# Linear attention and gated MLP on one core: a weight fold cut into quarters and queued behind products, and one load of raw weights moved

## The chip, the cores and the metric

The kernel runs on one core of a Trainium2 chip. The metric is the device time of one execution in microseconds (us). Before the change three runs gave 2350.81, 2344.51 and 2345.13 us, with a median of 2345.13 us.

## The reference

For an input `x` of 2048 rows by 1024 columns, all in 32-bit floats:

```python
xn = layernorm(x)
q, k, v = heads(xn @ wqkv)                       # 32 heads of 32
pq, pk = per_head(q @ w_phi), per_head(k @ w_phi)
phi(p) = concat(softmax(p), softmax(-p))         # 64 features a head
kv, z = phi(pk)^T v, sum_s phi(pk)
s = heads_back(phi(pq) kv / (phi(pq) z + 1e-6)) @ wo
g = silu((sigmoid(xn @ w_gate) * (xn @ w_up)) @ w_down)
out = x + s * g
```

The per-head matrices `w_phi` can be multiplied into the weights of q and k before the projection. The kernel calls this a **fold**: the product of a block of raw weights (`wqkT`) with a block-diagonal matrix made of `w_phi` (`bd`).

## The kernel before, in words

Every large product is cut into two by two blocks and done with seven block products in place of eight (`B11, B21, T2, T3, T4, T1, B22`, in this order); their operands are sums and differences of blocks. Each float is split into a high and a low part, so that one block product is three matmuls (`mm3`, lines L224 to L226; the startup's own lines are L1007). `split` makes the parts: a cast on ScalarE (L219, in the startup L928), then a subtraction on VectorE (L220, in the startup L931).

The 2048 rows are done in two chunks (`c` 0 and 1). Each chunk projects v, then k, then q, seven products each, and then does the gate and up products. One projection product is four tiles of rows (`u` 0 to 3) with 12 matmuls of 128 x 512 each; results pile up in four PSUM banks and are evacuated by `proj_out` (L506 on VectorE, L509 and L512 on ScalarE), which stores the finished ones with L503. The buffer of finished v tiles of T4 has two halves, so a third evacuation waits for the first store to land, and so on.

The startup is written out by hand as a long list of steps (`FIRST`). It covers the layer norm, the folds of k for the quarters k = 0, 1, 2 of the inner dimension, and the first five products of v in chunk 0 (B11 to T4). VectorE carries its evacuations, subtractions and sums in one queue.

The other five folds (k's fourth, and q's four) are put on the list `side`, whose entries are taken one for each tile of a projection product, from v's T1 on. A fold is done by `fold`: four loads of raw weights of 256 KB (L323), four groups of four 128 x 128 matmuls (`fold_products`, L329) into banks 4 to 7 (`bank_102` to `bank_105` in the listings), four copies out of PSUM on ScalarE (`fold_copy`: L339 for k, L337 for q), three stores of plain blocks to DRAM (`fold_keep`, L350), four sums on VectorE and GpSimd (`fold_sum`, L79), and four stores of sums. The raw weights lie in four buffers; a load waits until the group that read its buffer before is done. A projection product then loads its weights from DRAM (`prep`, L469, 1 MB, two buffers in turn) and splits them.

A scheduler places the instructions of the five engines' queues where it expects their inputs to be ready, so the written order binds only through data and through `tc.issue_after`, which keeps what stands under it behind a given instruction. SyncE (SP) issues all DMAs, in one queue.

Of the kernel before, what the change touches and what calls it, by code (L numbers as in the profile page):

```python
# [138 lines left out]
def hedgehog_glu_kernel(  # L139
# [176 lines left out]
    fraw = Ring(halves(43, 11))  # L316
    fblock = {K: Ring(((4, 5), (6, 7), (52, 53), (50, 51))), Q: Ring(((52, 53), (50, 51)))}

    folds, folded = {}, {}

    def fold_load(which, k, n, r=None):
        r = folds[which, k, n] = fraw.next() if r is None else r
        last_sp[:] = [nc.sync.dma_start(r, wqkT[which, n // 2, k + 4 * (n % 2)].rearrange("p g n -> p (g n)")).ins]  # L323
# [28 lines left out]
    def fold(which, k):  # L352

        for n in range(4):
            if (which, k, n) not in folds:
                fold_load(which, k, n)
        for n in range(4):
            fold_copy(which, k, n, fold_products(which, k, n, tps.next()))
        fold_keep(which, k, False)
        if k < 3:  # L360
            for n in range(4):
                fold_load(which, k + 1, n)
        for i in range(4):
            fold_sum(which, k, i, (vector, pool)[i % 2])
        with tc.issue_after(last_sp[0]):
            fold_keep(which, k, True)
# [84 lines left out]
    def prep():  # L451
        if flow["item"] == len(items):
            return False
        n, size = items[flow["item"]]
        if flow["made"] + size - flow["used"] > NW:
            return False
        w = 28 + flow["made"] % NW
        flow["item"] += 1
        flow["made"] += size
        kind, c, what, i = ops[n]  # L460
        if kind == "proj":
            h = len(ready[n]) // 2
            if h == 0:
                here = c == 0 and what == V
                proj_src[n] = r = v_first[i] if here else proj_raw.next()
                if what == V and i in (B11, B21, T4) and not (here and i != T4):
                    nc.sync.dma_start(row4(r), v_block(*{B11: (0, 0), B21: (0, 1), T4: (1, 1)}[i]))
                elif not here:
                    nc.sync.dma_start(row4(r), wf_d[what, i])  # L469
            o = run(w, 2)  # L470
            split((o[:, :, 0], o[:, :, 1]), slots[proj_src[n] + h])
            ready[n] += [w, w + 1]
            return True
        u = units.index((c, *what))
        if i == glu_order[0]:
            if u % (2 * NJ) == 0:
                glu_load(u)
            if (u + 1) % (2 * NJ):
                glu_load(u + 1)
            glu_sums(u)  # L480
        kept = ws_d[u % (2 * NJ), summed.index(i)] if i in summed else None
        if c and i in summed:
            last_sp[:] = [nc.sync.dma_start(slots[w].bitcast(F32), kept).ins]
        else:
            split(pair(w), wraw[u][i])
            if i in summed:
                nc.sync.dma_start(kept, slots[w].bitcast(F32))
        ready[n].append(w)
        return True
# [328 lines left out]
        if q:  # L818
            e_load(u)

    last_mm = []

    def numerators(tp_):

        sums = []
# [231 lines left out]
        pass  # L1057
    for n in range(4):
        fold_load(K, 3, n)
    side.append(lambda: None)  # L1060
    for w, k in [(K, 3)] + [(Q, k) for k in range(4)]:
        side.append(lambda w=w, k=k: fold(w, k))

    gmm = Ring(banks[:4])
    gbank = {}
# [57 lines left out]
    for n, (kind, c, what, i) in enumerate(ops):  # L1123
        ws = ready[n]
        if kind == "proj":
            if n < 5:
                continue
            for u in range(4):
                if i in opening:
                    pbank[u] = pmm.next()  # L1130
                xo = run(XO[i], 4)
                us = slice(u * P, (u + 1) * P)
                for k in range(4):
                    mm3(pbank[u], (xo[:, k, 0, us], xo[:, k, 1, us]), pair(ws[k]),
                        i in opening and k == 0, k == 3, skip_group_check=True)
                step()
                if c and operands.left:
                    operands.step()
            flow["used"] += 4
            while prep():  # L1140
                pass
            store_now(n)
            if c == 0 and what == Q and i == B11:
                block("p", 36, 3, F32R)
            assert what != Q or not c or not proj1.left and not operands.left
            for u in range(4):
                proj_out(c, what, i, u, pbank[u])
                if c == 0 and what == Q:
                    background(last_evac[0], early_k)
                elif c and not (what == V and i in (B11, B21)):  # L1150
                    if what != Q and u < 3 and proj1.left:
                        background(last_evac[0], proj1)
                    elif what == Q and i not in (B11, B21):
                        background(last_evac[0], late_k)
            continue

        j, s = what
        u = units.index((c, j, s))
        if (j, s, i) == (0, 0, 0):
            step(1000)  # L1160
        if i in opening:
            gbank[i] = gmm.next()
        bank = gbank[{B21: B11, T4: T3, B22: T1}.get(i, i)]
        w = [h.rearrange("p (k m) -> p k m", m=P) for h in pair(ws[0])]
        xo = run(XO[i], 4)
        for k in range(4):
            mm3(bank, (w[0][:, k], w[1][:, k]), (xo[:, k, 0], xo[:, k, 1]),
                i in opening and k == 0, k == 3, skip_group_check=True)
        flow["used"] += 1
        while prep():  # L1170
            pass
        last_unit = u == len(units) - 1
        if flow["item"] == len(items) and flow["made"] - flow["used"] < NW:
            hfree.append(ws[0])
            if last_unit and i == 0:
                wfree.extend(range(16, 20))
            while wfree and down_prep():
                pass
        if i == B11:
            u1, u2 = ur.next(), ur.next()  # L1180
            nc.scalar.copy(u1, bank)
        elif i == T2:
            v = nc.vector.tensor_add(u1, u1, bank)
        elif i == T3:
            v = nc.vector.tensor_add(u2, u1, bank)
        else:
            q = {B21: 0, T1: 3, T4: 2, B22: 1}[i]
            if s == 0:
                gates[q] = gates_free.popleft()
            g = gates[q]  # L1190
            if s == 0:
                if q == 0:
                    nc.scalar.activation(g, bank, AF.Sigmoid)  # L1193
                else:
                    v = nc.vector.tensor_add(g, u2 if q == 3 else u1, bank)
                    nc.scalar.activation(g, g, AF.Sigmoid)
            else:
                if q == 0:
                    nc.vector.tensor_mul(g, g, bank)
                else:  # L1200
                    b = u1 if q == 1 else u2
                    v = nc.vector.tensor_add(b, u2 if q == 3 else u1, bank)  # L1202
                    last_pool[:] = [pool.mul(g, g, b).ins]
                if q != 1:
                    later(n + 1 + (q > 0), h_d[(B11, None, B21, T4)[q], j, :, c], g)
                else:

                    a11, a21, a12, a22 = [gates[q] for q in range(4)]
                    s3, s2, s4 = [hs_r.next() for _ in range(3)]
                    pool.sub(s3, a11, a21)  # L1210
                    pool.add(a21, a21, a22)
                    pool.sub(s2, a21, a11)
                    pool.sub(s4, a12, s2)
                    for o, b in ((T3, s3), (T1, a21), (T2, s2), (B22, s4)):
                        later(n + 3, h_d[o, j, :, c], b)
                    gates_free.extend((a22, a11, a12, a21))

        store_now(n + 100 * (n == len(ops) - 1))
        m = (u % (2 * NJ)) * 7 + glu_order.index(i)
        if m > 1:  # L1220
            if c:
                paced(v.ins, beside1, 186 - m)
            elif early_k.left:
                background(v.ins, early_k)
            elif kv_due:
                kv_products()
            else:
                paced(v.ins, beside0, 187 - m)
        if c == 0 and u % (2 * NJ) == 2 * NJ - 1:
            for _ in range((1, 2, 2, 1, 1, 1, 1)[glu_order.index(i)]):  # L1230
                operands.step()
            if i == B22:
                block("p", 36, 3, F32R)
# [211 lines left out]
```

## Time and profile before

| | |
|---|---|
| median of three runs | 2345.13 us (2344.51 to 2350.81) |
| the profiled execution's own time | 2345.94 us |
| its span, from first to last instruction | 2343.9 us |
| TensorE (PE) busy | 2326.3 us, 99% of the span |
| VectorE (DVE), GpSimd (POOL), ScalarE (ACT) busy | 1636.9, 1111.7, 955.6 us |
| share of PE in the chain that ended last | 90% |

PE is busy nearly throughout, so the places to read are the few in which it waits. "Waits" lists sum what an engine waited for; the "chain" follows the work that ended last, step by step; the "timeline" shows instructions with start, duration and, in brackets, the idle time before them and what ended it. Matmul durations in the timeline overlap: the step from one to the next is 0.23 us at full clock.

### The profile page before, as it was taken

The numbers are of one execution on the slowest core, as the hardware profiler recorded it, in microseconds if no ns is written. First come the engines' busy times: TensorE is split into PE (matmuls) and PEld (weight loads), VectorE is DVE, ScalarE is ACT, GpSimd is POOL, SyncE is SP. The second block draws the span as 40 slices with busy tenths as digits, with TensorE's granted clock in tenths as the row PEclk, the third lists the DMA queues.
The fourth block names the chain that finished last, engine by engine and source line by source line (L and its number), as shares of the span: only waits on it lengthen the run. The fifth ranks groups of instructions, "written<-read, shape, count | busy, mean of one in ns | idle before, by whom it ended". The sixth has DMA issues, their size and how long they took to land.

```text
span 2343.9 us, 32067 instructions
## 1 busy us (share of the span) xinstructions
PE 2326.3 (99%) x10644; PEld 1922.1 (82%) x10644; DVE 1636.9 (70%) x2333; ACT 955.6 (41%) x1410; POOL 1111.7 (47%) x1270
## 2 busy tenths in 40 slices
PE   9999999999999999999999999999999999999999
PEld 8788888888888878888888888888888888887777
DVE  8735788677777666566867777865666777666765
ACT  7333354445544444333435344443434333344321
POOL 2210267777777643304364544645444445633444
PEclk9999999999999999999999999999999999999999
DMA  8775566888888889958888888879777877887774
GB/s 313 270 272 172 186 221 220 277 311 303 295 304 285 289 291 357 325 170 279 267 274 282 286 272 267 288 242 354 237 240 256 267 253 236 263 286 265 255 253 166
DMA packets 265414, 624.10 MB, mean 266 GB/s; under 512 B 36896, under 2 KB 65696, under 8 KB 260640
## 3 DMA queue, kind: packets, MB, share of 16 engines
q1 hardware_dynamic: 265248, 622.05, 77.8%
q8 instruction: 84, 1.38, 0.2%
q14 instruction: 82, 0.67, 0.1%
HBM read 373.42 MB, written 248.51 MB: 265 GB/s over the span
## 4 chain that ended last, share of the span: by engine, by line
PE 90%; DMA 3%; DVE 3%; POOL 1%; issue 1%; ACT 1%; SPq 0%; ACTq 0%; DVEq 0%; POOLq 0%
PE bank L224 29%; PE bank L225 29%; PE bank L226 28%; PE bank L602 1%; DMA fa<-w_down 1%; PE bank L834 1%; PE bank L1007 1%; PE bank L329 1%; POOL fc L79 1%; POOL fb L79 1%; DMA fa<-wv 1%; DMA fc<-xo_d 1%; DVE w L220 0%; ACT x L219 0%; DVE x L931 0%
## 5 line engine op out<-in xcount | busy, mean ns | idle before, releaser
L225 PE MATMUL bank<-x,w 128*128 128x512 f32 x2352 | 915.7, 389 | 1.9 <-DVE x L220 1.9
L224 PE MATMUL bank<-x,w 128*128 128x512 f32 x2352 | 906.8, 390 | 1.5 <-ACT fc L1193 1.0
L226 PE MATMUL bank<-x,w 128*128 128x512 f32 x2352 | 904.4, 389 | 0.0
L79 POOL TENSOR_TENSOR fc<-fc 128x256 f32<-128x256 f32 x436 | 376.8, 893 | 503.9 <-DMA fc<-e_d 112.5
L219 ACT CAST w<-fa 128x512 fp32r<-128x512 f32 (+1 forms) x436 | 299.6, 691 | 572.1 <-PE bank L225 367.0
L220 DVE TENSOR_TENSOR w<-fa,w 128x512 fp32r<-128x512 f32 (+1 forms) x436 | 398.6, 918 | 187.5 <-ACT w L219 175.6
L224 PEld LDWEIGHTS bank<-x,w 128*128 128x128 f32 x2352 | 441.5, 188 | 94.7 <-ACT fc L1193 1.8
L225 PEld LDWEIGHTS bank<-x,w 128*128 128x128 f32 x2352 | 441.6, 188 | 93.2 <-DVE x L220 2.7
L226 PEld LDWEIGHTS bank<-x,w 128*128 128x128 f32 x2352 | 441.5, 188 | 91.6
L224 PE MATMUL bank<-w,x 128*128 128x512 f32 x636 | 249.6, 393 | 2.1 <-DVE fc L506 0.6
L225 PE MATMUL bank<-w,x 128*128 128x512 f32 x636 | 249.2, 392 | 0.3 <-DVE w L931 0.3
L226 PE MATMUL bank<-w,x 128*128 128x512 f32 x636 | 248.8, 391 | 0.0
L79 POOL TENSOR_TENSOR fb<-fa 128x256 f32<-128x256 f32 x112 | 99.1, 905 | 213.7 <-DMA fa<-w_gu 120.8
L79 POOL TENSOR_TENSOR fb<-fb,fc 128x256 f32<-128x256 f32 x132 | 124.4, 962 | 119.3 <-DVE fc L1202 119.1
L224 PEld LDWEIGHTS bank<-w,x 128*128 128x128 f32 x636 | 119.9, 189 | 28.5 <-DVE fc L506 1.4
L79 POOL TENSOR_TENSOR fc<-fc,sa 128x256 f32<-128x256 f32 x128 | 96.8, 787 | 95.3 <-issue 86.8
L225 PEld LDWEIGHTS bank<-w,x 128*128 128x128 f32 x636 | 120.1, 189 | 25.5 <-DVE w L931 0.8
L226 PEld LDWEIGHTS bank<-w,x 128*128 128x128 f32 x636 | 120.1, 189 | 24.9
L219 ACT CAST p<-fc 128x512 fp32r<-128x512 f32 x96 | 73.1, 764 | 146.5 <-DVE fc L575 78.2
L1202 DVE TENSOR_TENSOR fc<-fc,bank 128x512 f32<-128x512 f32 x84 | 57.3, 682 | 93.6 <-PE bank L226 68.3
L220 DVE TENSOR_TENSOR x<-fa,x 128x512 fp32r<-128x512 f32 x112 | 90.9, 812 | 44.1 <-ACT x L219 43.8
L220 DVE TENSOR_TENSOR p<-fc,p 128x512 fp32r<-128x512 f32 x96 | 95.9, 1003 | 31.2 <-ACT p L219 31.1
(209 smaller groups left out, 2806.6 us busy)
## 6 DMA issues: line engine op xcount, KB each, us to landing
ws_d<-w SPq DMA_DIRECT2D x112, 512.0 KB, 4.2
w<-ws_d SPq DMA_DIRECT2D x112, 512.0 KB, 5.1
fa<-w_gu SPq DMA_DIRECT2D x84, 512.0 KB, 4.6
fa<-h_d SPq DMA_DIRECT2D x84, 512.0 KB, 5.1
fa<-wf_d SPq DMA_DIRECT2D x32, 1024.0 KB, 6.6
h_d<-fc SPq DMA_DIRECT2D x120, 256.0 KB, 4.6
fa<-w_down SPq DMA_DIRECT2D x80, 256.0 KB, 5.0
h_d<-fb SPq DMA_DIRECT2D x76, 256.0 KB, 4.4
```

Source lines behind the costliest of these rows:

```text
L79: last = self.engine.tensor_tensor(o[:, s], a[:, s], b[:, s], op=op)
L219: nc.scalar.copy(o[0], src)
L220: return nc.vector.tensor_sub(o[1], src, o[0].bitcast(F32))
L224: nc.tensor.matmul(o, a[0], b[0], start=first, stop=False, **kw)
L225: nc.tensor.matmul(o, a[0], b[1], start=False, stop=False, **kw)
L226: return nc.tensor.matmul(o, a[1], b[0], start=False, stop=last, **kw)
L329: nc.tensor.matmul(ps[:, gs], r[:, gs], bd[:, 4 * (n // 2) + g], start=True, stop=True)
L602: nc.tensor.matmul(kvb[g // 2][:, g % 2 * 256:g % 2 * 256 + 256], v[:, g].rearrange("p a f -> p (a f)"), ph[:, g].rearrange("p a f -> p (a ...
L834: m = nc.tensor.matmul(ps[bs, j * 256:(j + 1) * 256], kv[:, 2 * j + b, bs], ph[:, 2 * j + b], start=True, stop=True, skip_group_check=True)
L1007: nc.tensor.matmul(banks[u], xo[:, k, l, us], w[m], start=i in opening and k == 0 and a[3] == "a", stop=k == 3 and l == 1, skip_group_chec ...
L1202: v = nc.vector.tensor_add(b, u2 if q == 3 else u1, bank)
```

## The change

The fourth fold of k is no longer one call of `fold`. It becomes four calls of `fold_quarter` and one of `fold_sums`. A quarter's matmuls are put behind the last matmul of the newest projection tile (`last_mm`); the quarter is then copied out and, save for one of the four, stored at once. The list `side` becomes: nothing, quarter 0, nothing, quarters 1 to 3, the sums, and then q's four folds, the first of which stands five tiles later on the list than before. The loads keep their calls. The second part: when the raw weights of chunk 1's first v product (B11) are loaded, those of the second (B21) are loaded too, into the other buffer.

```diff
-    folds, folded = {}, {}
+    folds, folded, last_mm = {}, {}, []
...
+    def fold_quarter(which, k, n):
+        with tc.issue_after(last_mm[0]):
+            ps = fold_products(which, k, n, tps.next())
+        fold_copy(which, k, n, ps)
+        if n != 2:
+            i = (B11, B21, None, T4)[n]
+            nc.sync.dma_start(wf_d[which, i, :, k], folded[which, k][n])
+
+    def fold_sums(which, k):
         for i in range(4):
             fold_sum(which, k, i, (vector, pool)[i % 2])
         with tc.issue_after(last_sp[0]):
...
-            if h == 0:
+            if h == 0 and n not in proj_src:
...
+                if c and what == V and i == B11:
+                    proj_src[n + 1] = proj_raw.next()
+                    nc.sync.dma_start(row4(proj_src[n + 1]), v_block(0, 1))
...
-    side.append(lambda: None)
-    for w, k in [(K, 3)] + [(Q, k) for k in range(4)]:
-        side.append(lambda w=w, k=k: fold(w, k))
+    quarters = [lambda n=n: fold_quarter(K, 3, n) for n in range(4)]
+    side.extend([lambda: None, quarters[0], lambda: None] + quarters[1:] + [lambda: fold_sums(K, 3)])
+    for k in range(4):
+        side.append(lambda k=k: fold(Q, k))
...
-                    mm3(pbank[u], (xo[:, k, 0, us], xo[:, k, 1, us]), pair(ws[k]),
-                        i in opening and k == 0, k == 3, skip_group_check=True)
+                    m = mm3(pbank[u], (xo[:, k, 0, us], xo[:, k, 1, us]), pair(ws[k]),
+                            i in opening and k == 0, k == 3, skip_group_check=True)
+                last_mm[:] = [m.ins]
```

How the queues stand before and after is shown at three places. The first is PE's queue from the end of v's T3 over T4 (`x_1_611` is its operand) to the first matmuls of T1 (`x_1_787`). Before:

```order
L1007 MATMUL bank_101<-w_93,x_0_86 128x512 x4
L329 MATMUL bank_103<-fb_96 128x128 x4
L1007 MATMUL bank_99<-w_93,x_1_611 128x512 x8
L1007 MATMUL bank_98<-w_93,x_1_611 128x512 x12
L329 MATMUL bank_105<-fb_96,fc_97 128x128 x2
L1007 MATMUL bank_101<-w_93,x_1_611 128x512 x8
L1007 MATMUL bank_100<-w_93,x_1_611 128x512 x12
L1007 MATMUL bank_99<-w_93,x_1_611 128x512 x4
L1007 MATMUL bank_101<-w_93,x_1_611 128x512 x4
L329 MATMUL bank_105<-fb_96,fc_97 128x128 x2
L224 MATMUL bank_98<-w_93,x_1_787 128x512
L329 MATMUL bank_102<-fb_96 128x128 x4
```

and after, where L1022 is the line that was L1007:

```order
L1022 MATMUL bank_101<-w_93,x_0_86 128x512 x4
L1022 MATMUL bank_99<-w_93,x_1_611 128x512 x8
L1022 MATMUL bank_98<-w_93,x_1_611 128x512 x12
L1022 MATMUL bank_101<-w_93,x_1_611 128x512 x8
L1022 MATMUL bank_100<-w_93,x_1_611 128x512 x12
L1022 MATMUL bank_99<-w_93,x_1_611 128x512 x4
L1022 MATMUL bank_101<-w_93,x_1_611 128x512 x4
L224 MATMUL bank_98<-w_93,x_1_787 128x512
L224 MATMUL bank_101<-w_93,x_1_787 128x512
L224 MATMUL bank_100<-w_93,x_1_787 128x512
L224 MATMUL bank_99<-w_93,x_1_787 128x512
L225 MATMUL bank_98<-w_93,x_1_787 128x512
```

The groups of L329 are gone from this stretch. Before, six groups (24 matmuls) stood from the first matmuls of v's T3 to the fifth of T1: two among T3's matmuls, one ahead of T4, one in two halves within T4 and at its end, two among T1's first four. After, the first group stands 26 matmuls into T1, and all 20 groups of the five folds come from there on.

The second place is VectorE's queue at the end of T4, from the last two subtractions for T1's operand ahead of T4's evacuations (L506, after the change L523). Before:

```order
L220 TENSOR_TENSOR w_93<-fa_95,w_93 128x2x512
L506 TENSOR_TENSOR fc_97<-fc_97,bank_101 128x512
L931 TENSOR_TENSOR x_1_787<-fc_97,x_1_787 128x4x128
L506 TENSOR_TENSOR fc_97<-fc_97,bank_100 128x512
L931 TENSOR_TENSOR x_1_787<-fc_97,x_1_787 128x4x128
L220 TENSOR_TENSOR w_93<-fa_95,w_93 128x2x512
L506 TENSOR_TENSOR fc_97<-fc_97,bank_99 128x512
L931 TENSOR_TENSOR w_93<-p_94,w_93 128x2x512
```

and after (L946 is the line that was L931):

```order
L523 TENSOR_TENSOR fc_97<-fc_97,bank_101 128x512
L946 TENSOR_TENSOR x_1_787<-fc_97,x_1_787 128x4x128
L523 TENSOR_TENSOR fc_97<-fc_97,bank_100 128x512
L946 TENSOR_TENSOR x_1_787<-fc_97,x_1_787 128x4x128
L220 TENSOR_TENSOR w_93<-fa_95,w_93 128x2x512 x2
L523 TENSOR_TENSOR fc_97<-fc_97,bank_99 128x512
L946 TENSOR_TENSOR w_93<-p_94,w_93 128x2x512
```

Both splits of weights (L220) now stand behind the evacuations of banks 101 and 100. Ahead of this place VectorE's queue is unchanged.

The third place is PE's queue in k's first product, B11 (`x_0_90`), after the change. The four groups of q's first fold stand just ahead of B11's first matmul; this is the end of its first tile and the first group of q's second fold:

```order
L224 MATMUL bank_98<-w_93,x_0_90 128x512
L225 MATMUL bank_98<-w_93,x_0_90 128x512
L226 MATMUL bank_98<-w_93,x_0_90 128x512
L224 MATMUL bank_98<-w_93,x_0_90 128x512
L225 MATMUL bank_98<-w_93,x_0_90 128x512
L226 MATMUL bank_98<-w_93,x_0_90 128x512
L224 MATMUL bank_99<-w_93,x_0_90 128x512
L329 MATMUL bank_102<-fb_96 128x128 x4
L225 MATMUL bank_99<-w_93,x_0_90 128x512
```

That group stands 13 matmuls behind the four groups of the first fold, the first of which frees its raw buffer. Before, no more than three groups of these folds stood in a row. From about 150 us on no engine's queue differs between the two kernels, but for the line that names one load: at the start of chunk 1 the DMA at the place of the first load of raw v weights carries the change's new line, and the place, its waits and its neighbours are those of before.

## Rows read from the trace of the kernel before

**Rows 1.** The page, busy time: engine, us, share, instructions.
```profile
PE 2326.3 (99%) x10644; PEld 1922.1 (82%) x10644; DVE 1636.9 (70%) x2333; ACT 955.6 (41%) x1410; POOL 1111.7 (47%) x1270
```

**Rows 2.** PE's waits, 60 to 100 us: us in total, times, longest.
```profile
PE bank L329 <- DMA fc<-wqkT: 1.8, 2, 1.2
PE bank L1007 <- DVE fc L506: 0.7, 1, 0.7
PE bank L224 <- DVE fc L506: 0.6, 2, 0.4
PE bank L225 <- DVE w L931: 0.3, 1, 0.3
```

**Rows 3.** Chain that ended last, 60 to 104 us: start, us, what.
```profile
78.57 4.20 DMA fc<-wqkT
...
83.52 6.37 PE bank L1007 x28
...
90.80 3.54 DMA qkv_d<-fc
...
94.43 0.69 DVE fc L506
95.12 1.15 DVE w L931
...
96.31 0.79 PE bank L225
...
101.80 0.27 PE bank L226
102.07 0.23 PE bank L224
```

**Rows 4.** Timeline of DVE: start, us, line, operation [idle before, releaser].
```profile
72.57 1.23 DVE L931 TENSOR_TENSOR w<-fa,w 128x1024 fp32r<-128x1024 f32 x1 [1.44 <-ACT w L928]
...
80.69 1.28 DVE L506 TENSOR_TENSOR fb<-fc,bank 128x512 f32<-128x512 f32 x2
...
89.94 0.69 DVE L506 TENSOR_TENSOR fc<-fc,bank 128x512 f32<-128x512 f32 x1
...
92.34 1.22 DVE L220 TENSOR_TENSOR w<-fa,w 128x1024 fp32r<-128x1024 f32 x1
94.43 0.69 DVE L506 TENSOR_TENSOR fc<-fc,bank 128x512 f32<-128x512 f32 x1 [0.87 <-DMA qkv_d<-fc]
```

**Rows 5.** Timeline of PE, the startup and v's T1.
```profile
67.39 9.36 PE L1007 MATMUL bank<-w,x 128*128 128x512 f32 x40 [0.75 <-DVE fc L506]
76.60 1.05 PE L329 MATMUL bank<-fb 128*128 128x128 f32 x8
...
103.95 0.39 PE L225 MATMUL bank<-w,x 128*128 128x512 f32 x1
104.18 1.05 PE L329 MATMUL bank<-fb,fc 128*128 128x128 f32 x8
104.99 0.48 PE L226 MATMUL bank<-w,x 128*128 128x512 f32 x1
105.31 0.40 PE L224 MATMUL bank<-w,x 128*128 128x512 f32 x1
```

**Rows 6.** Stretches: us, PE, PEld, DVE, ACT, POOL busy (count), granted clock, DMA share, GB/s.
```profile
92.00:94.90 2.90, 1.51 (x9) 1.03 (x9) 2.03 (x3) 0.00 (x0) 0.00 (x0) 1.00 1.00 374
96.30:101.70 5.40, 5.39 (x13) 4.23 (x14) 0.29 (x1) 1.17 (x2) 0.00 (x0) 0.50 1.06 362
```

**Rows 7.** The page, DMA issues: KB each, median us to landing.
```profile
fa<-wf_d SPq DMA_DIRECT2D x32, 1024.0 KB, 6.6
...
wf_d<-fc SPq DMA_DIRECT2D x42, 256.0 KB, 5.5
```

**Rows 8.** The loads of raw weights for folds, L323, in the view by line.
```profile
DMA to landing us min/median/max: 2.6/5.5/10.2
```

**Rows 9.** Timeline of PE at chunk 1's first product of v.
```profile
829.16 0.73 PE L224 MATMUL bank<-w,x 128*128 128x512 f32 x2 [0.62 <-ACT w L219]
```

More of the change, by code (lines that the diff above doesn't have):

```diff
@@ L362, in fold @@
                 fold_load(which, k + 1, n)
+        for i in range(4):
+            fold_sum(which, k, i, (vector, pool)[i % 2])
+        with tc.issue_after(last_sp[0]):
+            fold_keep(which, k, True)
+    def fold_quarter(which, k, n):
[6 more added lines that the diff above has]
+    def fold_sums(which, k):
         for i in range(4):
@@ L819, in phi_transpose @@
             e_load(u)
-    last_mm = []
     def numerators(tp_):
```

## The prediction

> **What bounds the kernel now.** The busy times come first: PE works 2326.3 of 2343.9 us [rows 1]. So a change can win only where PE waits or runs slowly, and whatever it adds to PE elsewhere costs its full length. The change touches the time up to about 150 us, and behind 96.31 us the view of waits shows no wait of PE there. So I read PE's waits up to 100 us [rows 2]: two for raw weights of folds (1.8 us) and four for VectorE (1.6 us), 3.4 in all. The stretches add the clock: it is granted in full up to 94.9 us; from 96.3 to 101.7 us it is 0.50, that is 1.2 in place of 2.4 GHz, while PE works without a pause; in the 2.9 us ahead, PE was busy for 1.51 [rows 6]. In the chain twelve matmul steps from 96.31 to 101.80 took 5.49 us; from 102.07 on a step takes 0.23 [rows 3], and twelve are 2.76, so the slow clock cost 2.7 us.
>
> The chain also says what the waits hang on [rows 3]. T4's second half starts behind a group of a fold, whose raw weights land only at 82.77; then come 28 matmuls; then T4's last evacuation waits for the store of another tile (90.80 to 94.34); then the last split of T1's weights ends at 96.27, and PE goes on at 96.31. Beside this VectorE is full: from 72.57 on it has little idle time up to 93.6 [rows 4].
>
> **The change, part by part.** *Six groups leave the startup.* By the queues, 24 fold matmuls that stood ahead of 96.31 now stand behind it. One group's price is read where PE runs at full speed: the matmul ahead of it starts at 103.95, the second behind it at 105.31 [rows 5]; of these 1.36 us two plain steps are 0.46, so a group costs 0.90. Six cost **5.4 us**, and there is no wait behind 96.31 to hide them. What they gave in the startup has to be worked out.
>
> *When PE goes on with T1.* Without the fold's wait, T4's second half needs bank 101 to be evacuated; that is the second of the two evacuations at 80.69, done at 81.97 [rows 4]. The 28 matmuls take 6.37 us [rows 3], to 88.34, in place of 89.9. VectorE reaches the evacuation of bank 101 at about 88.4, since a split that stood ahead now stands behind. Evacuation, subtraction, evacuation, subtraction took from 89.94 to 92.34, 2.4 us [rows 4]; two splits at 1.2 us follow, to 93.2. The store that the last evacuation waits for is issued at about 89.2 and takes 3.54 us [rows 3], to 92.8, so it no longer decides. Evacuation and split, 0.69 and 1.15 us, end at 95.0. So PE resumes at 95.0 in place of 96.3: **-1.3 us**. All six groups leave, but only 1.3 us come back, because VectorE's queue is the next thing late; the rest turns into idle time of PE. Bounds: 0, if a delay further up (next part) reaches through, and -1.6, T4's own gain.
>
> *The clock.* The six groups partly filled waits. At 67.39 PE waited 0.75 us for VectorE [rows 5]; two groups stood in the 6 us ahead, so some 2.5 us of idle time in a row will stand there. Ahead of the restart it grows to 95.0 - 88.4 less four steps, 5.7 us. What the rows show: single waits of 0.6 and 0.75 us were followed by no lower clock, and 1.4 us of idle time within 2.9 was [rows 2, 6]. At the restart I therefore take the same slow stretch as before, 0; bounds -2.7 (none) and +0.8 (PE at work in the slow stretch a little longer). At 67.39 a fall would slow T3's 40 matmuls by up to 2.7 us, so T4 starts at 76.6 + 2.7 = 79.3. Its 48 matmuls (11.0 us) would end at 90.3 in place of 88.4: +1.9. The trace has no such pause, so the ends are 0 and +1.9; I take the middle, **+1.0**. The Trainium skill (TensorE: Matmul & The Clock Gate, "Loop structure matters more than you think") says that matmuls kept back to back keep the clock, and that waits in between let it fall to half. This speaks against a change that takes matmuls out of waits, and by it the sum holds the full +1.9; the trace agrees at 94.9 us, and no row shows it for a pause like that at 67.39.
>
> *New waits.* The group of q's second fold that needs a load soonest stands behind four groups and 13 matmuls; its buffer is free after the first of the four. Groups in a row take 0.81 each (104.18 to 104.99) [rows 5], so 3 x 0.81 + 13 x 0.23 = 5.4 us lie between. Such loads land after 2.6 to 10.2 us, median 5.5 [rows 8]. The wait is 0 to 4.8 us, by the median 0.1; SP has a store ahead of the load that waits for VectorE, so I take **+0.4**.
>
> *K's first weights* now hang on the first quarter: its group 22 steps behind the restart, half of them slow, ends at about 103.7; a copy and the store's 5.5 us, then the load's 6.6 [rows 7] and the splits, give about 120.5. PE gets there after 92 matmuls, eight groups and the slow stretch: 95.0 + 21.2 + 7.2 + 2.7 = 126. The cost is 0, with 5 us to spare; beyond that each microsecond counts in full. SP has no more DMAs than before, and a store of a quarter no longer stands ahead of v's.
>
> *The second load of chunk 1* stands at the same place of SP's queue as before, with the same waits: 0. If it did come earlier, it could not win more than the 0.62 us that PE waits there [rows 9].
>
> **Sum:** 5.4 - 1.3 + 1.0 + 0 + 0.4 = 5.5 us. The profiled execution took 2345.94, so 2351.4; that run lies 0.8 above the median of the runs, 2345.13, against which I state the forecast: **2350.6 us**, 0.23% above. A measurement of this kernel tells 0.3%, 7.0 us, from no change, so this counts as the same. With all costs at their low ends, 5.4 - 1.6 - 2.7 = +1.1, 2346.2; at their high ends it passes 2356.
>
> **The rivals.** *All waits vanish.* If VectorE has room, PE resumes T1 without a pause and the clock stays up: the waits behind 82 us (2.7 of the 3.4) and the 2.7 go, and the six groups, which were PE's work anyway, cost nothing: 2339.7. For it: the chain runs over a fold's load for 4.2 us. Against it: VectorE's full queue from 72.57. Chance 0.10.
>
> *The clock falls twice, and long.* +1.9 at 67.39 and +0.8 at the restart: 5.4 - 1.3 + 1.9 + 0.8 + 0.4 = 7.2, 2352.3. For it: both pauses are longer than the one that was followed by half clock. Against it: T4's start has slack to take some. Chance 0.18.
>
> *Slower: the load for q's second fold is late.* Groups of folds stand closer together, and loads of 1 MB run beside them (the DMA share at 96 to 101 us is already 1.06 [rows 6]). The place is the second tile of k's B11. From a landing of 7.3 us on, the total is over 7 us; at 10.2 us it is 4.8 + 5.4 - 1.3 + 1.0 = 9.9, 2355.0. For it: before, the two waits of this kind cost 1.8 us [rows 2]. Against it: behind 96 us none did. Chance 0.13.
>
> *The change does nothing.* If the groups were not held back, 2345; the queues say that they are. Chance 0.03. The forecast has 0.56.
>
> **How the numbers follow.** The range of 2345 to 2355.5 leaves out the first rival and little at the top. Faster by over 0.3% (below 2338.1) needs more than the first rival gives: 0.03. Slower (above 2352.2): the third rival, half of the second and a little of the forecast: 0.25. Between: 0.72.
>
> **What would show it.** PE's waits between 60 and 97 us grow to about 8 us, all of them for VectorE or ScalarE and none for raw weights; T1's stream resumes at 95 to 96 us; fold groups between 100 and 150 us rise by six; behind the stream's start PE shows no wait but one at k's B11. The forecast is wrong if T1 resumes before 93 us, if no stretch shows a clock of 0.50, or if PE waits over 2 us behind 100 us.

## The result and the profile after

22 runs of the changed kernel gave a median of 2352.08 us (2348.57 to 2358.19), 22 of the kernel before 2345.3 us (2342.47 to 2353.47). The ratio is 1.0029, with a 95% interval of 1.0021 to 1.0038: some 7 us slower. The interval leaves out 1, so the loss is clear of the scatter, and it lies at the edge of the 0.3% that the forecast calls the same. The profiled execution after the change took 2355.67 us, among the slower of its 22; its span is 2353.9 us.

The page's busy times, which answer to [rows 1]:

```profile
PE 2329.2 (99%) x10644; PEld 1925.6 (82%) x10644; DVE 1636.8 (70%) x2333; ACT 956.1 (41%) x1410; POOL 1113.6 (47%) x1270
```

As many instructions on each engine, and PE 2.9 us more busy. PE's waits from 60 to 100 us, to set beside [rows 2] (us in total, times, longest):

```profile
PE bank L224 <- DVE fc L523: 4.2, 3, 3.0
PE bank L1022 <- DVE fc L523: 2.2, 1, 2.2
PE bank L225 <- DVE w L946: 0.3, 1, 0.3
```

The two waits for raw weights are gone, and 3.4 us of waits have become 6.7, all for VectorE. From 100 to 200 us, where before had none, two waits are new:

```profile
PE bank L329 <- DMA fb<-wqkT: 1.8, 1, 1.8
PE bank L329 <- DMA fc<-wqkT: 0.4, 1, 0.4
```

PE's timeline at the same places as [rows 5] (start, us, line, operation, in brackets the idle time before and what ended it):

```profile
68.76 20.82 PE L1022 MATMUL bank<-w,x 128*128 128x512 f32 x88 [2.20 <-DVE fc L523]
...
95.02 0.80 PE L224 MATMUL bank<-w,x 128*128 128x512 f32 x1 [2.97 <-DVE fc L523]
96.16 0.79 PE L225 MATMUL bank<-w,x 128*128 128x512 f32 x1 [0.34 <-DVE w L946]
...
129.59 1.05 PE L329 MATMUL bank<-fb 128*128 128x128 f32 x8
133.62 1.13 PE L329 MATMUL bank<-fb 128*128 128x128 f32 x8 [1.84 <-DMA fb<-wqkT]
135.11 1.97 PE L329 MATMUL bank<-fb,fc 128*128 128x128 f32 x8 [0.36 <-DMA fc<-wqkT]
```

From T3's stream on, 88 matmuls run without a fold between them; T1 resumes at 96.16. Absolute times mislead by 1.4 us here: T3's stream starts at 68.76 instead of 67.39. In that execution PE waited 2.7 us for the first rows of x in place of 1.3, and the clock was at half behind that wait (shown below the table); how much each of them shifts the start is not shown. The second and third groups of q's second fold wait at 133.62 and 135.11. The stretches (us, PE, PEld, DVE, ACT, POOL busy, granted clock, DMA share, GB/s) show what the clock did at T3's start, at the restart of T1, and (the last three) at q's second fold:

```profile
67.40:76.60 9.20, 7.84 (x35) 6.50 (x35) 7.81 (x12) 3.04 (x4) 1.98 (x3) 1.00 0.92 290
96.16:101.00 4.84, 4.84 (x11) 3.80 (x12) 0.00 (x0) 0.00 (x0) 0.00 (x0) 0.50 0.20 76
132.00:134.00 2.00, 0.38 (x3) 0.41 (x4) 0.00 (x0) 0.00 (x0) 0.00 (x0) 1.00 0.97 358
134.00:136.00 2.00, 1.64 (x11) 1.48 (x11) 0.00 (x0) 0.00 (x0) 0.00 (x0) 0.80 1.06 351
136.00:138.00 2.00, 2.00 (x9) 1.81 (x8) 0.69 (x1) 0.58 (x1) 0.45 (x1) 0.50 1.14 289
```

It stayed at 1.00 behind the 2.20 us wait of T3, was 0.50 at the restart as before [rows 6], and fell again behind the waits for q's raw weights. What made these late stands in SP's queue (its waits from 105 to 134 us, then its timeline):

```profile
SPq L350 <- DVE fc L79: 4.2, 1, 4.2
...
SPq L350 <- POOL fc L79: 2.2, 1, 2.2
```

```profile
125.83 0.32 SPq L350 DMA_DIRECT2D wf_d<-fc  x1
126.24 0.74 SPq L323 DMA_DIRECT2D fb<-wqkT  x1
129.29 0.79 SPq L350 DMA_DIRECT2D wf_d<-fc  x2
130.18 0.40 SPq L323 DMA_DIRECT2D fb<-wqkT  x1
```

L350 stores the sums of k's fourth fold. SP waits 4.2 us for a sum on VectorE and 2.2 for one on GpSimd, and the load for the second quarter of q's second fold, issued at 130.18, stands behind; the group that reads it starts at 133.62.

**Three marks.** Executions of one kernel differ by several us, so I compare stages within profiles: A, the start of T3's stream behind its wait; B, the first L225 of T1; C, the first product with v. C is the row

```profile
252.17 1.12 PE L602 MATMUL bank<-p 128*128 128x256 f32 x8
```

before, and after the change

```profile
261.50 1.12 PE L619 MATMUL bank<-p 128*128 128x256 f32 x8
```

From B to C I sum, over stretches of 1 us, PE's idle time and the time that the slow clock took ((1 - granted clock) x busy time), and subtract both. What is left is work. From C to the end ten of the twelve profiles lie between 2089.1 and 2093.1 us (before 2091.7, after 2092.4); the two others are told of at the end. What happens ahead of A is not in these numbers. All numbers in us:

| kernel | A to B | B to C | slow clock | waits | left, against before | A to C, against before | median against before |
|---|---|---|---|---|---|---|---|
| before | 28.92 | 155.86 | 2.72 | 0 | 0 | 0 | 0 |
| the change | 27.40 | 165.34 | 4.16 | 2.19 | +5.85 | +7.96 | +6.8 |
| the change, again | 27.46 | 163.45 | 2.72 | 1.39 | +6.20 | +6.13 | +10.2 |
| part 1 only | 28.44 | 161.98 | 1.23 | 1.25 | +6.36 | +5.64 | +6.7 |
| q spread | 28.44 | 161.55 | 1.42 | 0.57 | +6.42 | +5.21 | +6.9 |
| sums later | 28.47 | 160.24 | 1.64 | 0 | +5.46 | +3.93 | +4.1 |
| two in the gap | 28.46 | 168.20 | 3.41 | 7.14 | +4.51 | +11.88 | +13.2 |
| groups twice | 29.00 | 163.20 | 2.97 | 0 | +7.09 | +7.42 | +7.6 |
| part 2 only | 28.88 | 154.85 | 1.61 | 0 | +0.10 | -1.05 | +0.1 |
| idle groups | 27.27 | 159.51 | 0 | 0.53 | +5.84 | +2.00 | +5.3 |
| two real | 29.71 | 158.50 | 1.71 | 0 | +3.65 | +3.43 | +3.2 |
| two real, two idle | 27.21 | 157.42 | 0 | 0.26 | +4.02 | -0.15 | +4.1 |

**The clock over all runs.** The table has one execution of each kernel. But every run lists its mean granted clock, to three digits, and (1 - granted clock) x span is what the slow clock took in it. Its mean is 6.2 us over the 22 runs of the change and 3.2 to 3.5 us over the runs of the kernel before (17 to 35 runs in three sessions); it is 5.7 us for sums later and 3.5 us for idle groups, 12 runs each. By the scatter of the runs, such a mean is good to about 0.5 us. So the slow clock takes some 3 us more after the change. Between A and C the seven profiles of the new order without idle groups show only about 1 us of it. The rest seems to lie outside the marks: both profiles of the change run at half clock near 12 us, and sums later and two real do so near 500 us, while no profile with before's order (before, groups twice, part 2 only) does at either place. Why the change should move the clock there is not shown. The stretch near 12 us, before and after the change:

```profile
12.40:15.60 3.20, 3.20 (x21) 2.44 (x20) 3.16 (x6) 2.94 (x5) 0.00 (x0) 1.00 1.03 391
```

```profile
12.40:15.60 3.20, 3.20 (x15) 3.01 (x14) 3.00 (x5) 2.94 (x5) 0.00 (x0) 0.50 1.04 393
```

### The profile page after: what moved, and what is told of

Same layout as the page of the kernel before. It is cut to its first block, busy times and chain, and to the rows that moved or that the text cites. A ratio compares the mean times of both kernels' runs of the same rounds, so it can differ in the third digit from the quotient of the medians.

```text
span 2353.9 us, 32070 instructions
## 1 busy us (share of the span) xinstructions
PE 2329.2 (99%) x10644; PEld 1925.6 (82%) x10644; DVE 1636.8 (70%) x2333; ACT 956.1 (41%) x1410; POOL 1113.6 (47%) x1270
## 4 chain that ended last, share of the span: by engine, by line
PE 86%; DMA 5%; issue 3%; DVE 3%; POOL 2%; ACT 1%; SPq 0%; ACTq 0%; DVEq 0%; POOLq 0%
PE bank L224 27%; PE bank L226 27%; PE bank L225 27%; PE bank L619 1%; POOL fc L79 1%; PE bank L1022 1%; PE bank L849 1%; PE bank L329 1%; POOL fb L79 1%; DVE w L220 1%; DMA fc<-xs_d 0%; DMA fc<-xo_d 0%; DMA fa<-w_down 0%; PE bank L1004 0%; DMA x<-wo_d 0%
## 5 line engine op out<-in xcount | busy, mean ns | idle before, releaser
L225 PE MATMUL bank<-x,w 128*128 128x512 f32 x2352 | 917.0, 390 | 1.6 <-DVE x L220 1.5
L220 DVE TENSOR_TENSOR w<-fa,w 128x512 fp32r<-128x512 f32 (+1 forms) x436 | 398.3, 917 | 177.0 <-ACT w L219 162.4
L225 PEld LDWEIGHTS bank<-x,w 128*128 128x128 f32 x2352 | 441.9, 188 | 92.9 <-DVE x L220 2.8
L225 PE MATMUL bank<-w,x 128*128 128x512 f32 x636 | 249.6, 392 | 0.3 <-DVE w L946 0.3
L225 PEld LDWEIGHTS bank<-w,x 128*128 128x128 f32 x636 | 120.5, 189 | 25.4 <-DVE w L946 0.8
L220 DVE TENSOR_TENSOR x<-fa,x 128x512 fp32r<-128x512 f32 x112 | 92.9, 829 | 49.1 <-ACT x L219 49.1
L220 DVE TENSOR_TENSOR p<-fc,p 128x512 fp32r<-128x512 f32 x96 | 97.3, 1018 | 31.8 <-ACT p L219 31.7
```

Source lines behind the costliest of these rows:

```text
L220: return nc.vector.tensor_sub(o[1], src, o[0].bitcast(F32))
L225: nc.tensor.matmul(o, a[0], b[1], start=False, stop=False, **kw)
```

## The experiments

The theory: six groups moved from waits that VectorE set into PE's full stretch, a wait for raw weights came new, and the clock fell once more; the second part does nothing. The rivals: the second part is the cause, or the groups cost less and a new wait makes the loss.

**Part 1 only.** The second part's prefetch is taken out:

```diff
-            if h == 0 and n not in proj_src:
+            if h == 0:
...
-                if c and what == V and i == B11:
-                    proj_src[n + 1] = proj_raw.next()
-                    nc.sync.dma_start(row4(proj_src[n + 1]), v_block(0, 1))
```

> The change without its second part: the raw weights of chunk 1's second product load where they did before. Theory (the whole difference is made before 140 us of the span: six groups at 0.90 us = +5.4, a restart of T1 earlier by 1.4, a 2.2 us wait at q's second fold and about 1.8 us of half clock behind it): as the whole change, +6.8 us over before, within 1. Rival A (the second part costs or gives something of its own, up to the 0.62 us wait on ACT that is gone from 829 us): +7.4 at most. Rival B (the second part is the cause of the loss): within 1 of before.

2352.05 us, ratio 1.0033 (1.0022 to 1.0045): the same as the whole change. Its profile also shows the fall of the clock at T3 that the first profile of the change did not. Set beside the row at 68.76 above (L1019 is L1022 there):

```profile
66.41 21.86 PE L1019 MATMUL bank<-w,x 128*128 128x512 f32 x88 [2.21 <-DVE fc L520]
```

The same 88 matmuls behind the same wait took 1.04 us more, and B came that much later behind A.

**Part 2 only.** The same lines, put into the kernel before.

> The kernel before with the second part of the change alone: the raw weights of chunk 1's second product of v loaded in one call with the first's. Theory (same place of SP's queue, nothing waits for it but 0.62 us at 829 us): within 1 us of before, the wait on ACT at 829 us there or not. Rival (the earlier load pushes others back): +1.5 or more.

2345.18 us, ratio 0.9996 (0.9983 to 1.0009). With the run above, the second part costs and gives nothing that the medians can tell; the interval here is -4.0 to +2.1 us. One small thing goes with it: the wait for ScalarE at chunk 1's first product of v (0.62 us in [rows 9]) stands in all three profiles without the second part, 0.6 to 1.0 us long, and in one of the nine with it.

**Groups twice**, in the kernel before:

```diff
+            r, ps = folds[which, k, n], tps.next()
+            if which == Q and k > 1:
+                fold_products(which, k, n, ps)
+                folds[which, k, n] = r
-            fold_copy(which, k, n, fold_products(which, k, n, tps.next()))
+            fold_copy(which, k, n, fold_products(which, k, n, ps))
```

> The kernel before, with each of the eight groups of q's third and fourth folds issued twice into the same bank (the second product has the same result). They stand where TensorE runs without a wait at full clock. Theory (a group costs its whole length there, 0.90 us, or 0.81 in a row): eight more groups give +6.5 to +7.2 us over before, all of it ahead of the first product with v (252.2 us in before), and nothing else moves. Rival (TensorE's stretch hides part of it, so that the six groups of the change cost less than 5.4 us): +4 or less.

2352.68 us, ratio 1.0029 (1.0016 to 1.0041). C stands here:

```profile
258.62 1.11 PE L606 MATMUL bank<-p 128*128 128x256 f32 x8
```

From B to C 7.34 us more, 7.09 without the clock: 0.89 us for each of eight groups. The price of a group is shown, and the rival of hidden groups falls by the profile. The median, +7.6, is a little above the +6.5 to +7.2 that I expected; its interval, +3.8 to +9.6, holds both, and would not settle it alone.

**q spread**: each of q's folds is followed by two empty entries of the list.

```diff
     for k in range(4):
         side.append(lambda k=k: fold(Q, k))
+        side.extend([lambda: None] * 2)
```

> The whole change, with each of q's four folds followed by two empty entries of the side list, so that every fold comes three steps behind the one ahead of it. Theory (the load of q's second fold was 2.2 us late and the clock fell behind that wait): no PE wait for raw weights between 100 and 160 us, clock 1.00 from 101 us on, and the time falls by 3.5 to 4.2 us: +2.6 to +3.3 over before. Rival A (the six groups alone make the loss; wait and clock fall are made up by something later): stays at +6 to +7.5. Rival B (spreading makes q's weights late for their first product, a new wait past 150 us): +4 or more, with that wait in the list.

2352.18 us, ratio 1.0030 (1.0018 to 1.0042). The waits behind B fell to 0.57 us and the clock stayed up, yet the time is that of the change: my -3.5 to -4.2 was wrong. I had taken the wait and the fall of the first profile for the rule.

**Sums later**: the sums stand behind q's first fold.

```diff
-    side.extend([lambda: None, quarters[0], lambda: None] + quarters[1:] + [lambda: fold_sums(K, 3)])
-    for k in range(4):
+    side.extend([lambda: None, quarters[0], lambda: None] + quarters[1:])
+    side.append(lambda: fold(Q, 0))
+    side.append(lambda: fold_sums(K, 3))
+    for k in range(1, 4):
```

> The whole change, with the sums of k's fourth fold moved behind q's first fold in the side list, so that the stores of those sums no longer stand ahead of the loads of q's second fold in SP's queue; the distance between q's folds stays one step. Theory (the loads are late because SP first waits for the sums on VectorE and GpSimd, 3.9 us of wait in the chain): no PE wait, or less than 0.5 us, at q's second fold; the clock stays at 1.00; +2.6 to +3.5 over before. Rival A (one step between two folds is too short for a load whatever the queue does): the wait stays at 1.8 us or more, time +6 to +7.5. Rival B (the wait moves to q's third fold, whose loads now stand behind those stores): a wait of 1 to 3 us one fold later, +5 to +7.

2349.44 us, ratio 1.0021 (1.0010 to 1.0032); no wait of PE from 100 to 160 us. In SP's timeline the loads now come one after the other:

```profile
119.88 0.42 SPq L323 DMA_DIRECT2D fb<-wqkT  x1
120.40 0.40 SPq L350 DMA_DIRECT2D wf_d<-fc  x1
120.90 0.38 SPq L323 DMA_DIRECT2D fb<-wqkT  x1
121.37 0.38 SPq L350 DMA_DIRECT2D wf_d<-fc  x1
121.84 1.54 SPq L323 DMA_DIRECT2D fc<-wqkT  x2
```

First and second load are 1.0 us apart, where the change had 3.9. The edit does one thing more: the entry of the sums now stands between q's first two folds, so their groups are 21 matmuls apart in place of 13. That alone is not what helped. In this run the second load had landed 7.6 us behind the start of the first fold's first group (118.60 to 126.21); in the change the group that reads it was due 8.7 us behind that start (123.05 to 131.78). By this estimate it would have come in time at the old distance too. So the cause of the late load is the stores of k's sums in SP's queue. The median is +4.1 where I expected +2.6 to +3.5, and 2.6 us below that of the change; its interval, +2.3 to +7.5 us over before, would not settle it alone.

**Two in the gap**: quarters 0 to 2 are queued behind the startup's last product, q's folds spread (the loop of the startup also sets `last_mm`).

```diff
-    quarters = [lambda n=n: fold_quarter(K, 3, n) for n in range(4)]
-    side.extend([lambda: None, quarters[0], lambda: None] + quarters[1:] + [lambda: fold_sums(K, 3)])
+    for n in range(3):
+        fold_quarter(K, 3, n)
+    side.extend([lambda: None] * 2 + [lambda: fold_quarter(K, 3, 3), lambda: None, lambda: fold_sums(K, 3)])
```

> Quarters 0 and 1 of the fold queued on TensorE behind the last product of the startup and ahead of T1, where TensorE waits for VectorE anyway; quarters 2 and 3 in T1; q's folds spread by two empty entries each as in the run with spread folds. Theory (a group is worth 0.90 us only where it lies in TensorE's full stretch; in the gap it is free): two groups less than the run with spread folds, so 1.8 us less than that run: +0.8 to +1.5 over before. Rival A (VectorE or ScalarE, which copy the quarters out and split T1's operands, set the restart, and copies in the gap delay it): no better than the run with spread folds. Rival B (a group in the gap also shortens the slow clock behind the restart, since TensorE idles less): 1 us better still, 0 over before.

2358.50 us, ratio 1.0058 (1.0042 to 1.0074): none of my cases. The two groups in the gap did not move B (28.46 us behind A, as without them), but one line of PE's waits from 100 to 200 us says where the time went:

```profile
PE bank L329 <- DMA fb<-wqkT: 7.1, 3, 3.0
```

Raw weights late again, three times, this time with the folds far apart. SP's waits from 120 to 162 us point to the same cause, now with the sums of q's own folds (the last store of k's sums was issued at 117.9):

```profile
SPq L350 <- DVE fc L79: 9.0, 2, 4.5
SPq L350 <- POOL fc L79: 5.6, 2, 3.1
```

The three loads that PE waited for, issued at 133.38, 136.31 and 153.27 behind such stores, then took 6.6 to 9.3 us to land. Why this held PE up here and hardly in q spread, where q's folds stand as far apart, is not shown.

**Two real**: the run with sums later, with quarters 0 to 2 behind the third of T1's first matmuls (`head` is the first matmul of `mm3`).

```diff
+                    if n == 5 and (u, k) == (2, 0):
+                        last_mm[:] = head
+                        for f in range(3):
+                            fold_quarter(K, 3, f)
...
-    side.extend([lambda: None, quarters[0], lambda: None] + quarters[1:])
+    side.extend([lambda: None] * 5 + quarters[3:])
```

> The run with the sums later, with quarters 0 to 2 of the fold queued behind the third of T1's first matmuls: by the queues two groups then stand in the 2.97 us wait ahead of T1, and one 26 matmuls on. Theory (a group is free in a wait that VectorE sets, and costs 0.90 us in the full stretch; with 1.7 us of the wait filled the clock may stay up): two groups come back, 1.8 us less than the run with the sums later, and up to 1.6 more if the clock stays: +0.7 to +2.3 over before. Rival A (their copies and stores push q's loads back as in the run with two quarters in the gap): a wait of 2 us or more for raw weights, +5 to +12. Rival B (the copies on ScalarE delay T1's operands): T1 resumes more than 28.6 us behind T3's start.

2348.29 us, ratio 1.0014 (0.9999 to 1.0029); no late weights. PE's timeline at the gap:

```profile
92.14 1.95 PE L329 MATMUL bank<-fb 128*128 128x128 f32 x16
95.27 0.50 PE L224 MATMUL bank<-w,x 128*128 128x512 f32 x1 [1.19 <-DVE fc L523]
96.40 0.50 PE L225 MATMUL bank<-w,x 128*128 128x512 f32 x1 [0.63 <-DVE w L946]
```

The two groups (16 records) fill 1.78 of the 2.97 us, and VectorE still ends the wait. Behind B four of the six groups remain, and the work left is +3.65, 0.91 each: a group costs its length in the full stretch and nothing in the wait. The clock fell at T3 (A to B 29.71) and at B all the same, and the median, +3.2, is above the +0.7 to +2.3 that I expected.

**Idle groups**: the run with sums later, plus groups that nothing reads, two in the wait ahead of T3's stream and three in the one ahead of T1.

```diff
+    def idle_groups(count):
+        for j in range(count):
+            for g in range(4):
+                nc.tensor.matmul(banks[7 - j % 2][:, g * P:(g + 1) * P], bd[:, g], bd[:, g], start=True, stop=True)
...
+            if what == "mm T3 3 0 a":
+                with tc.issue_after(last_mm[0]):
+                    idle_groups(2)
...
+                    if n == 5 and (u, k) == (2, 0):
+                        with tc.issue_after(head[0]):
+                            idle_groups(3)
```

> The run with the sums later, plus five groups of products of bd with itself that nothing reads: two in the 2.2 us wait ahead of T3's matmuls (63 to 67 us) and three in the 2.97 us wait ahead of T1. Theory (the clock fell behind these two waits, which cost 1.04 us in T3 and T4 and 1.6 us behind the restart, and idle time of TensorE is free): clock 1.00 from 60 to 150 us, T3's 88 matmuls in 20.8 us in place of 21.9, time 2.7 us less than the run with the sums later: +1.4 over before. Rival A (the groups delay the waiting matmuls): no gain, +4 or more. Rival B (VectorE sets the restart whatever the clock does): only the 1.6 us behind the restart come back, +2.5.

2350.40 us, ratio 1.0020 (1.0006 to 1.0034). PE's timeline (L335 is the line of these groups, L1030 that of the stream), and the stretch behind B:

```profile
65.71 1.95 PE L335 MATMUL bank<-fb 128*128 128x128 f32 x16
67.96 20.82 PE L1030 MATMUL bank<-w,x 128*128 128x512 f32 x88 [0.30 <-DVE fc L528]
...
92.11 2.84 PE L335 MATMUL bank<-fb 128*128 128x128 f32 x24
...
95.23 0.50 PE L225 MATMUL bank<-w,x 128*128 128x512 f32 x1
```

```profile
95.20:101.00 5.80, 5.76 (x28) 4.88 (x29) 1.14 (x2) 0.00 (x0) 0.00 (x0) 1.00 0.49 170
```

The clock is 1.00 at all three places; A to B is 1.20 us shorter than in the run with sums later, and the slow stretch behind B is gone. So work in the waits keeps the clock up, and not in this execution alone: over 12 runs the slow clock took 3.5 us, against 5.7 with sums later. From A to C that is 1.93 us in the profile (3.93 to 2.00). The medians don't show it (+5.3 against +4.1), so something else took it back, and what is open.

**Two real, two idle**: the run with two real quarters and the two idle groups at T3.

> The run with two real quarters in the wait ahead of T1, plus two of the groups that nothing reads in the 2.2 us wait ahead of T3's matmuls. Theory (the wait ahead of T3 lets the clock fall in most executions, for 1.0 to 2.3 us): T3's 88 matmuls take 20.8 us, T1 resumes 27.3 us behind T3's start, four groups stand behind the restart; up to the first product with v -1.6 + 3.6 - 1.1 = +0.9 us against before, and the time 1 to 2 us below the run with two real quarters: within 1.5 us of before. Rival (the clock there does not hang on that wait): T3 and T4 slow as before, no gain.

A to B is 27.21 us as expected, and from A to C the profile is as fast as before (-0.15); the median is 2348.92 us, ratio 1.0018 (1.0004 to 1.0031). The two disagree, and I leave that open. The clock stayed up at the restart too, where the same two real groups fill the wait as in "two real", and there it fell: the filling of that wait alone does not decide it. No version that I tried beats the kernel before.

**The change, again.**

> The whole change once more, for a second profile. Theory (the 2.2 us wait and the half clock at q's second fold in the first profile were one execution's; the wait there is 0.5 to 1.3 us as in the runs with part 1 alone and with spread folds): T3 and T4 at half clock for about 1 us of loss, a wait of 0.5 to 1.5 us for raw weights behind 120 us, no half clock behind it, +6 to +7.5 over before. Rival (the first profile is the rule): a wait of 2 us or more, and the clock at 0.5 behind it.

Six runs, median 2355.02 us, ratio 1.0040 (1.0025 to 1.0054); +10.2 is above the +6 to +7.5 that I expected, and the interval, +5.9 to +12.7, reaches down into it. PE's waits from 100 to 200 us:

```profile
PE bank L329 <- DMA fb<-wqkT: 0.8, 1, 0.8
PE bank L329 <- DMA fc<-wqkT: 0.6, 2, 0.4
```

1.4 us in place of 2.2, and no slow clock behind it: the fall at 134 us was one execution's, the wait is not. At T3 this execution again kept its clock (20.88 us for the 88 matmuls), against my expectation.

## Why the prediction was right or wrong

The forecast was +5.5 us (2350.6), measured was +6.8 (2352.08), within its range. That the two lie so close is in part luck: the load's wait and the clock took more than their terms, and on its second visit the same kernel measured +10.2. By its steps:

*Six groups, +5.4: right.* The work left between B and C is 5.5 to 6.4 us with six groups moved, 3.7 to 4.5 with four, 7.1 with eight added. The excess over 0.90 us a group stands mostly in the profiles that also have waits.

*PE goes on with T1, -1.3: right where the clock holds.* A to B is 27.4 us against 28.9 in both profiles of the change, -1.5. VectorE's queue is the next thing late, as forecast: 2.97 and 0.34 us of waits for it ahead of B.

*The clock at T3, +1.0 between 0 and +1.9: the middle holds.* The wait there is 2.2 us in every profile of the new order without idle groups. The clock fell behind it in five of these seven; in four that cost 1.04 us up to B, in "two real" 2.3, above the upper end, and in both profiles of the change nothing. The mean is 0.9. The Trainium skill (TensorE: Matmul & The Clock Gate, "Loop structure matters more than you think") lets the clock drop to half where a long wait for a DMA stands ahead of every matmul. One wait of 2.2 us for VectorE is not that case, so the +1.9 that the prediction drew from it was the prediction's own step; here the clock fell in five traces and not in two.

*The clock at the restart, 0: about right.* The slow clock took 2.72 us behind B before, 2.4 and 2.72 in the two profiles of the change; part 1 only, q spread, sums later and two real have 1.2 to 1.7, and a run with before's own queues there (part 2 only) has 1.61. So it scatters by itself.

*The clock as a whole: too small.* Its two terms make +1.0, and over all runs the slow clock takes some 3 us more than before. About 1 us of this lies between A and C, where the sum looked. The rival in which the clock falls twice, and long (2352.3) is nearer to the median than the forecast, but not by its mechanism: where the clock fell at T3, it took less behind B (1.2 to 1.7 us), not more.

*The load for q's second fold, +0.4: the step that was wrong.* It measured 2.2 and 1.4 us, and once a second fall of the clock, 1.7 us. I had reckoned the first quarter's load from when its buffer is free, and gave the store ahead of it 0.3 us beyond the median landing. It was the second quarter that was late, by SP's queue: behind stores of sums that wait on VectorE and GpSimd. The run with sums later shows it. The distance was also read a little short: groups in a row take 0.89 us (from 123.05 to 124.83 for two, in the change), not 0.81, which makes the 5.4 us 5.7. The rival "the load for q's second fold is late" named the right place, and the wait from which it decides, 1.9 us (a landing of 7.3 less 5.4), was passed in the first profile.

*K's first weights and the second part, 0 each: right.* No wait stands at k's B11 for them, and the two runs on the second part show no effect within their intervals of about 3 us to either side.

Of what I had said would show it: waits of "about 8 us" were 6.7, all for VectorE; T1 resumed at 96.16. "PE waits over 2 us behind 100 us", named as a sign that the forecast is wrong, came true in one profile of two: the sign pointed at the load's term, which was wrong, while the total stayed in the range.

What stays open: the medians of 12 runs have intervals of 2.6 to 3.5 us to either side, and three kernels (the two with idle groups at T3, and the change on its second visit) are 3 to 4 us slower against before in the median than in their profiles from A to C.

## What to carry to other kernels

Work on a nearly full engine is free only inside waits that another engine sets; before taking it out of them because it waits for a load itself, find out what ends the wait next, and price the work in the full stretch. When work is cut into pieces with stores of their own, follow the one queue that issues all DMAs: a store that waits for a sum holds every load behind it. Work taken out of waits can also cost clock, and the granted clock of all runs shows that better than one profile. Where executions differ by more than the effect, compare marks within profiles and take a second profile before explaining a wait of one.

## What the runs showed of the hardware

**The same wait, two outcomes.** PE waited 2.20 or 2.21 us ahead of T3's stream in seven profiles; the clock fell in five and not in two. The two without a fall are those in which the stream starts latest (68.76 and 68.35 us; the others 66.41 to 67.74). The same two had run at half clock near 12 us, and none of the five had. The length of a wait alone did not decide. The two profiles with idle groups at T3 had that early stretch too, so at T3 the profiles do not separate the groups from it; the clock over all runs (5.7 against 3.5 us) speaks for the groups.

**A starved VectorE.** In two of twelve profiles (sums later, two real) PE waits 4.2 and 4.6 us near 500 us, where before its only wait is 0.3. In the run with sums later, one subtraction on VectorE, then GpSimd's sums, then PE:

```profile
493.09 7.80 DVE L220 TENSOR_TENSOR w<-fa,w 128x512 fp32r<-128x512 f32 x1
```

```profile
491.95 2.83 POOL L79 TENSOR_TENSOR fb<-fb,fc 128x256 f32<-128x256 f32 x4
494.73 1.45 POOL L79 TENSOR_TENSOR fc<-fc,fb 128x256 f32<-128x256 f32 x2
496.11 1.45 POOL L79 TENSOR_TENSOR fb<-fb,fc 128x256 f32<-128x256 f32 x2
497.51 2.83 POOL L79 TENSOR_TENSOR fc<-fb,fc 128x256 f32<-128x256 f32 x4
```

```profile
504.32 0.53 PE L224 MATMUL bank<-x,w 128*128 128x512 f32 x1 [4.21 <-DVE fc L1204]
```

The subtraction ends at 500.9 us, half a microsecond behind the last of the ten sums that GpSimd started after it, without a pause. Before, the same subtraction took 0.84 us, and four sums beside it took 3.73 instead of 2.83, so there each seems to have had its turn:

```profile
490.38 0.84 DVE L220 TENSOR_TENSOR w<-fa,w 128x512 fp32r<-128x512 f32 x1
```

```profile
489.23 3.73 POOL L79 TENSOR_TENSOR fb<-fb,fc 128x256 f32<-128x256 f32 x4
```

The Trainium skill (SBUF — State Buffer, "SBUF: two separate sides") says that a VectorE operation with two SBUF inputs and a GpSimd operation that reads SBUF need one shared port pair, and that whichever starts first has it for its whole instruction while the other waits. The traces fit this: the subtraction has two inputs in SBUF and did not end before the sums did. If it is the port, the loser missed its turn through ten instructions; no run here tests that. Behind that wait the clock fell too, which took about 1.6 us in the run with sums later. It is a part of the scatter between executions, and the two profiles that show it have the longest time from C to the end, 2095.4 and 2100.5 us.
